# Loading and transposing q and k of the first two head sets in two parts, values sharing a PSUM bank, scrap products ahead, and new instruction orders in a fused attention and MLP kernel

## The chip, the cores and the metric

The kernel runs on one core of a Trainium2 chip. The metric is device time in microseconds (us) of one execution; lower is better. The kernel before has a median of 329.98 us over three runs.

## The reference

```python
def _attn_ref(q, k, v, beacon_k, beacon_v):          # B, H, S, D = 8, 8, 576, 64; 16 beacons
    k_all = np.concatenate([beacon_k, k], axis=2)
    v_all = np.concatenate([beacon_v, v], axis=2)
    scores = 1/sqrt(D) * q @ k_all^T                   # causal over k, beacons always seen
    a = softmax(scores)
    return a @ v_all
def _moe_ref(x, w_in, w_out):                          # 4608 tokens, 512 -> 2048 -> 512
    h = x @ w_in
    g = h * (1.0 / (1.0 + np.exp(-1.702 * h)))
    return g @ w_out
```

The attention output of all heads, as 4608 tokens of 512 values, is the input of the two-layer MLP.

## The kernel before

**Sets and chunks.** A set is four heads of one batch: two sets to a batch, 16 in all. Within a set the four heads run side by side in four strips of TensorE's rows or columns. The scores of a set (keys on partitions, queries along the row; only blocks that the causal mask leaves) have 1664 columns per head. They are made in chunks (`CHUNKS`): `e_qk` writes one chunk to the single PSUM tile `s`, `e_exp` (ScalarE) turns it into weights `E` in SBUF, and the next chunk may overwrite `s` only after that. The blocks on the diagonal are masked by VectorE for the first two sets (`e_mask`, tiles `keep` and `keepb`) and by GpSimd for the later ones.

**Values.** `e_av` multiplies `E` by a tile of ones (`x == 2`, the sums) and by the even and odd value columns (`x` 0 and 1), into one of four PSUM banks `u0` to `u3`, the ring. VectorE transposes the sums (`zt`), takes reciprocals (`rc`), spreads them (`rz`) and scales the values into `xT`, the transposed input of the MLP (`e_norm`). Sets below `EARLY` (the first four) are split into two halves of queries at `HF`; there each of the two value products has a bank of its own in both halves. Later sets share a bank for the two products in their first half.

**MLP.** `e_m1` makes 512 columns of the hidden layer in a ring bank; groups 0 and 1 (256 tokens each) take tanh on ScalarE and a product on VectorE (`e_tanh`, `e_gate`), later groups (512 tokens) take a table function (`e_gelu`). The second layer is `e_m2` for groups 0 and 1 and for the rest seven products in place of eight (`e_prod`), joined by VectorE. ScalarE changes its function table between exponentials and `e_gelu`.

**Loads.** q and k of a set lie in DRAM as four heads of 576 rows. `e_load_qk` brings them in float16 to `qn` or `kn`, 18 rows to a partition, and `e_turn` transposes them to `qT`, `kT` in one VectorE instruction. The loads of q, k, v and both weights are all issued by GpSimd (`pool_load`, with at most 8 in flight: a load waits until the one eight places ahead has landed). The beacons of k (`bkf`) come through SyncE's and ScalarE's queues, are cast to `bkn` and transposed into the first columns of `kT`.

**Order.** Instructions are first recorded as operations, and `ORDER` holds, written out for every engine, the numbers of the operations in the sequence in which they are issued. `Plan.run` only merges these five lists and assigns the ring's banks, for which it uses estimated durations. Each engine works through its list in order and waits on semaphores. The first entries are: loads of k, q of set 0, then k, q of set 1; then the mask tiles on GpSimd; then v and the weights. Chunk 0 is set 0's first half, chunk 1 set 1's first half, chunks 2 to 4 the rest of set 0, 5 to 7 the rest of set 1.

The lines that hold the loads and the transposes:

```python
HF = S // 2                                   # 288
def rows_of(t, s):
    return t[b, Q * hs : Q * hs + Q].rearrange("h (r t) d -> (h r) (t d)", t=TR)   # TR = 18
load_bk(0, 1, (), ("SP", "ACT"))
load_bk(1, HS)
load_qk(0, 1); load_qk(0, 0); load_qk(1, 1); load_qk(1, 0)
```

Of the kernel before, what the change touches and what calls it, by code (L numbers as in the profile page):

```python
# [17 lines left out]
        76, 100, 106, 138, 115, 141, 118, 143, 120, 108, 111, 155, 152, 129, 161, 158, 122, 131, 164, 167, 134, 127,  # L18
        170, 173, 176, 145, 125, 148, 150, 177, 182, 188, 191, 227, 194, 197, 232, 183, 203, 234, 200, 178, 237,
        179, 206, 258, 241, 209, 184, 263, 185, 212, 265, 213, 248, 246, 268, 214, 215, 401, 251, 253, 272, 218,  # L20
        404, 275, 244, 279, 219, 220, 407, 282, 284, 277, 221, 414, 320, 296, 304, 290, 302, 292, 300, 298, 312,
        308, 294, 318, 314, 310, 306, 316, 426, 435, 423, 343, 338, 339, 340, 433, 431, 438, 344, 345, 359, 349,
        341, 464, 346, 350, 351, 352, 354, 574, 355, 429, 360, 361, 577, 356, 362, 357, 372, 365, 583, 474, 477,
        373, 366, 374, 367, 605, 480, 484, 375, 482, 607, 368, 506, 502, 488, 492, 610, 490, 486, 498, 504, 500,
        508, 514, 510, 516, 494, 496, 512, 534, 593, 596, 535, 536, 539, 540, 550, 541, 542, 537, 742, 545, 546,
        547, 548, 603, 745, 551, 552, 553, 599, 601, 619, 622, 748, 555, 556, 557, 558, 561, 755, 625, 627, 629,
        562, 563, 776, 568, 564, 569, 570, 571, 779, 764, 767, 659, 637, 641, 657, 649, 651, 647, 661, 635, 631,
        653, 805, 772, 770, 774, 643, 655, 633, 639, 645, 679, 680, 815, 818, 700, 681, 682, 684, 701, 915, 690,
        685, 686, 691, 692, 702, 918, 687, 693, 695, 703, 696, 924, 821, 823, 697, 698, 706, 946, 825, 707, 713,
        708, 709, 948, 934, 937, 714, 715, 716, 827, 951, 944, 940, 942, 853, 831, 833, 855, 857, 851, 843, 835,  # L30
        837, 847, 839, 845, 829, 849, 841, 1083, 960, 963, 875, 876, 880, 877, 878, 881, 882, 1086, 968, 966, 970,
        883, 1089, 902, 909, 903, 886, 891, 1096, 887, 888, 889, 892, 893, 1117, 904, 894, 905, 896, 897, 1120, 898,
        899, 910, 911, 1105, 1108, 1146, 912, 976, 994, 996, 972, 978, 1000, 992, 982, 974, 998, 990, 984, 988, 980,
        1002, 986, 1256, 1156, 1113, 1111, 1115, 1159, 1025, 1020, 1026, 1021, 1259, 1022, 1027, 1031, 1023, 1028,
        1265, 1164, 1162, 1166, 1041, 1042, 1287, 1036, 1047, 1032, 1048, 1033, 1037, 1038, 1034, 1039, 1289, 1054,
        1055, 1049, 1056, 1043, 1044, 1050, 1292, 1057, 1198, 1172, 1168, 1178, 1184, 1180, 1194, 1170, 1174, 1176,
        1275, 1278, 1182, 1186, 1196, 1188, 1190, 1281, 1301, 1285, 1283, 1304, 1216, 1217, 1221, 1192, 1222, 1227,
        1218, 1223, 1228, 1219, 1224, 1232, 1229, 1233, 1230, 1307, 1311, 1309, 1237, 1327, 1333, 1238, 1243, 1234,
        1244, 1235, 1323, 1239, 1245, 1250, 1251, 1341, 1240, 1246, 1252, 1253, 1337, 1405, 1315, 1331, 1343, 1411,
        1335, 1321, 1403, 1431, 1313, 1325, 1407, 1419, 1317, 1423, 1425, 1319, 1339, 1421, 1409, 1329, 1361, 1413,  # L40
        1366, 1382, 1429, 1362, 1363, 1401, 1367, 1364, 1427, 1368, 1383, 1372, 1369, 1373, 1374, 1375, 1388, 1377,
        1389, 1378, 1390, 1395, 1379, 1384, 1380, 1385, 1391, 1396, 1415, 1397, 1398, 1470, 1454, 1417, 1455, 1449,
        1471, 1450, 1451, 1476, 1452, 1456, 1477, 1457, 1478, 1460, 1461, 1462, 1463, 1465, 1466, 1467, 1468, 1472,
        1479, 1473, 1483, 1484, 1485, 1486,
    ],
    "ACT": [
        1, 3, 77, 79, 103, 101, 107, 109, 112, 153, 156, 130, 159, 162, 132, 165, 168, 135, 171, 174, 189, 192, 228,
        195, 198, 233, 235, 201, 204, 238, 180, 207, 259, 210, 264, 186, 266, 269, 216, 402, 405, 408, 222, 417,
        415, 297, 291, 303, 305, 301, 299, 293, 309, 321, 295, 319, 313, 315, 311, 307, 317, 436, 439, 342, 465,
        468, 575, 578, 584, 587, 606, 608, 503, 507, 489, 491, 493, 487, 499, 505, 509, 515, 517, 495, 501, 511,  # L50
        497, 513, 611, 538, 743, 746, 749, 756, 758, 777, 780, 660, 642, 638, 652, 658, 648, 650, 636, 632, 662,
# [48 lines left out]
        1140, 1142, 1130, 1128,  # L100
    ],
    "SP": [
        0, 2, 4, 5, 6, 7, 83, 84, 85, 86, 88, 89, 90, 91, 181, 93, 94, 95, 96, 187, 217, 223, 348, 364, 371, 377,
        544, 560, 567, 573, 689, 705, 712, 718, 885, 901, 908, 914, 1030, 1046, 1053, 1059, 1226, 1242, 1249, 1255,
        1371, 1387, 1394, 1400, 1459, 1475, 1482, 1488,
    ],
# [89 lines left out]
def kernel(  # L196
# [66 lines left out]
    for t in kT:  # L263
        nc.vector.memset(t[:, NK:, :], 0.0)
# [855 lines left out]
```

The softmax here doesn't subtract the row's maximum and nothing guards it: scores larger than these inputs give would overflow.

## Time and profile before

| what | value |
|---|---|
| three runs | 329.98, 332.08, 329.78 us (median 329.98) |
| the profiled execution, first to last instruction | 328.1 us, granted TensorE clock 1.000 |
| TensorE (PE) busy | 309.3 us, 94% |
| VectorE (DVE) busy | 235.9 us, 72% |
| ScalarE (ACT) busy | 202.0 us, 62% |
| GpSimd (POOL) busy | 114.0 us, 35% |
| written by DMA over the span | mean 88 GB/s, 126 to 209 in the first seven of 40 slices |

The profile gives the span of its execution and no other time for it; the median of the runs is 1.88 us above that span, which is what lies around the first and the last instruction. PE is matrix multiplication, PEld the load of its weights. "L434 PE s" is the product of line 434 that writes tile `s`. Idle time of an engine that is not on the path that sets the end costs nothing.

### The profile page before, as it was taken

What the parts mean: (1) busy time and instruction counts of PE and PEld (TensorE: products, weight loads), DVE (VectorE), ACT (ScalarE), POOL (GpSimd) and SP (SyncE); (2) the same over time, 40 slices, a digit from 0 to 9 for tenths busy, and PEclk for the clock granted to TensorE, in tenths of its full rate; (3) what the DMA queues carried; (4) which work ended last, traced back from release to release, by engine and by line L of the source; (5) the groups of instructions that cost most, each with busy time, mean ns of one, the idle gap of its engine ahead of it and who ended that gap; (6) DMA issues with size and microseconds to landing.
All of it is one profiled execution on the core that took longest, in us unless ns stands there. A gap on an engine that the chain in (4) does not pass through costs nothing.

```text
span 328.1 us, 9811 instructions
## 1 busy us (share of the span) xinstructions
PE 309.3 (94%) x4288; PEld 210.0 (64%) x4288; DVE 235.9 (72%) x478; ACT 202.0 (62%) x236; POOL 114.0 (35%) x178
## 2 busy tenths in 40 slices
PE   0489999999999999999999999999999999999995
PEld 0367665544775467745878878547764776447884
DVE  3657788777987989977998798958557843006674
ACT  1567597687767686679767686868477212674010
POOL 8765487190319312951078019400042000000000
PEclk9999999999999999999999999999999999999999
DMA  7999999194424921693029809600120012000122
GB/s 126 161 202 209 203 187 181 34 99 103 113 67 72 186 50 34 70 191 57 2 45 177 133 2 122 157 0 2 37 96 2 2 34 78 18 0 2 65 98 97
DMA packets 58219, 28.81 MB, mean 88 GB/s; under 512 B 41280, under 2 KB 53568, under 8 KB 58176
## 3 DMA queue, kind: packets, MB, share of 16 engines
q0 software_dynamic: 47552, 18.49, 47.8%
q1 hardware_dynamic: 10560, 9.69, 9.1%
q8 instruction: 33, 0.54, 0.7%
q14 instruction: 10, 0.08, 0.1%
q10 hardware_dynamic: 64, 0.01, 0.0%
HBM read 37.22 MB, written 9.44 MB: 142 GB/s over the span
## 4 chain that ended last, share of the span: by engine, by line
PE 89%; ACT 4%; DVE 3%; DMA 2%; issue 1%; POOL 0%; DVEq 0%; ACTq 0%; POOLq 0%
PE u L580 36%; PE u L694 30%; PE s L434 9%; PE u L521 9%; PE u L625 4%; ACT E L445 3%; DMA qn<-in_q_dram 2%; DVE qT L405 1%; DVE sA L645 1%; DVE xT L556 1%; DVE rz L544 0%; DVE zt L533 0%; ACT L601 0%; DVE osb L710 0%; DVE rc L540 0%
## 5 line engine op out<-in xcount | busy, mean ns | idle before, releaser
L580 PE MATMUL u<-xT,w 128*128 128x512 f16 (+1 forms) x704 | 130.4, 340 | 0.5 <-ACT g L601 0.5
L445 ACT ACTIVATE E<-s 128x2048 f16<-128x2048 f32 (+5 forms) x66 | 98.9, 1515 | 46.0 <-PE s L434 45.6
L601 ACT ACTIVATE g<-u 128x512 f16<-128x512 f32 x128 | 70.5, 598 | 53.8 <-PE u L580 53.4
L580 PEld LDWEIGHTS <-w 128*128 128x128 f16 x704 | 67.8, 98 | 53.9 <-issue 1.5
L466 POOL TENSOR_SCALAR_AFFINE_SELECT E<-E 128x512 f16<-128x512 f16 (+3 forms) x78 | 49.3, 663 | 113.4 <-ACT E L445 81.6
L710 DVE SCALAR_TENSOR_TENSOR osb<-u,osb 128x512 f32<-128x512 f32 x56 | 37.2, 682 | 24.7 <-PE u L694 22.4
L694 PEld LDWEIGHTS <-g 128*128 128x128 f16 x512 | 48.4, 98 | 9.3 <-issue 0.2
L694 PE MATMUL u<-w,g 128*128 128x256 f16 x384 | 50.6, 273 | 0.0
L434 PE MATMUL s<-qT,kT 32*128 32x32 f16 (+20 forms) x1376 | 35.4, 232 | 14.4 <-DVE qT L405 8.4
L434 PEld LDWEIGHTS <-kT 32*128 32x128 f16 x1376 | 25.8, 94 | 30.6 <-issue 15.0
L694 PEld LDWEIGHTS <-sA 128*128 128x128 f16 x384 | 36.3, 98 | 5.3 <-issue 0.3
L694 PE MATMUL u<-tB,sA 128*128 128x256 f16 x256 | 35.0, 273 | 0.1
L645 DVE TENSOR_TENSOR sA<-g 128x512 f16<-128x512 f16 x32 | 12.9, 415 | 26.2 <-ACT g L601 26.2
L556 DVE TENSOR_TENSOR xT<-u,rz 128x352 f16<-128x352 f32 (+2 forms) x52 | 25.6, 517 | 6.9 <-PE u L521 6.7
L365 POOL DMA_DIRECT2D vb<-in_v_dram x32 | 27.4, 874 | 2.3 <-DMA kn<-in_k_dram 1.5
L521 PE MATMUL u<-E,vb 128*32 128x352 f16 (+8 forms) x928 | 28.0, 267 | 0.0
L484 DVE TENSOR_TENSOR zs<-zs,E 128x1344 f16<-128x1344 f16 (+2 forms) x36 | 22.7, 633 | 5.3 <-POOL E L466 4.4
L521 PEld LDWEIGHTS <-vb 128*32 128x32 f16 (+1 forms) x928 | 20.2, 99 | 5.9 <-issue 1.7
L405 DVE STREAM_TRANSPOSE kT<-kn 128x576 f32<-128x576 f32 x16 | 20.1, 1258 | 2.4 <-DMA kn<-in_k_dram 1.6
L405 DVE STREAM_TRANSPOSE qT<-qn 128x576 f32<-128x576 f32 x16 | 19.8, 1239 | 0.1
L533 DVE STREAM_TRANSPOSE zt<-u 128x224 f32<-128x224 f32 (+2 forms) x32 | 14.9, 471 | 6.6 <-PE u L521 6.5
L484 DVE TENSOR_TENSOR zs<-E 128x1856 f16<-128x1856 f16 x12 | 15.8, 1319 | 3.3 <-POOL E L466 3.3
(44 smaller groups left out, 237.7 us busy)
## 6 DMA issues: line engine op xcount, KB each, us to landing
out_dram<-osb SPq DMA_DIRECT2D x36, 256.0 KB, 2.5
kn<-in_k_dram POOLq DMA_DIRECT2D x16, 288.0 KB, 6.7
qn<-in_q_dram POOLq DMA_DIRECT2D x16, 288.0 KB, 6.6
vb<-in_v_dram POOLq DMA_DIRECT2D x24, 128.0 KB, 6.6
w<-in_moe_w_in_dram POOLq DMA_DIRECT2D x8, 256.0 KB, 9.9
w<-in_moe_w_out_dram POOLq DMA_DIRECT2D x4, 512.0 KB, 14.2
vb<-in_v_dram POOLq DMA_DIRECT2D x8, 112.0 KB, 5.0
vb<-in_v_dram POOLq DMA_DIRECT2D x8, 80.0 KB, 7.9
```

What stands on the lines that cost most here:

```text
L365: nc.gpsimd.dma_start(out=t[0 : hi - lo, j, h0:h1, :], in_=v[b, h0:h1, lo:hi, :].rearrange("h n d -> n h d"),)
L405: nc.vector.transpose(out=f32(dst.rearrange("p n e -> p (n e)")).rearrange("p (r t) -> p t r", t=TR), in_=f32(src[:, :]).rearrange("p (t c ...
L434: nc.tensor.matmul(sc[:, h, o : o + w], kT[s % NB2][r : r + 32, j * P : (j + 1) * P, d], qT[s % NB2][r : r + 32, a : a + w, d], start=(d = ...
L445: nc.scalar.activation(out=Es[s][:, :, c0:c1], in_=ss[i][:, :, o : o + c1 - c0], func=AFT.Exp, scale=0.125,)
L466: nc.gpsimd.affine_select(out=blk, in_=blk, compare_op=ALU.is_ge, fill=0.0, base=off + (Nb if j == 0 else 0), pattern=[[0, Q], [1, w]], ch ...
L484: nc.vector.tensor_tensor(out=t, in0=E[:, :, Z0:S] if i == 1 else t, in1=E[:, :, wcol[i] : wcol[i] + S - a], op=ALU.add,)
L521: nc.tensor.matmul(u[32 * h : 32 * h + 32, a:e], lhs, src[0:kw, h, col : col + e - a], start=first, stop=last,)
L556: nc.vector.tensor_tensor(out=xT[:, 2 * hs + x : 2 * hs + x + n, t0 : t0 + w], in0=rings[("av", s, x, half)][:, 0 : n * w].rearrange("p (n ...
L580: nc.tensor.matmul(u[:, o + a - t0 : o + e - t0], w1t[:, kp, nt * P : (nt + 1) * P], xT[:, kp, a % XR : (e - 1) % XR + 1], start=(kp == 0) ...
L601: nc.scalar.activation(out=gts[g][:, n0:n1, 0:w], in_=rings[("m1", g, n0)][:, 0 : n * w].rearrange("p (n w) -> p n w", n=n), func=AFT.Gelu ...
L694: nc.tensor.matmul(u[:, HM * mt : HM * (mt + 1)], lhs[:, n, mt * P : (mt + 1) * P], rhs[:, n, :], start=(n == 0 and mt == 0), stop=(n == H ...
L710: nc.vector.scalar_tensor_tensor(out=osbs[(g, dst)][:, :], in0=rings[("p", g, p)][:, :], scalar=scale_of(g), in1=osbs[(g, src)][:, :], op0 ...
```

## The change

1. `HF` becomes 256. The first half of an early set is queries 0 to 255; for batch 0 these are exactly the tokens of MLP group 0. The four chunks of an early set have 416 columns each (before: 512, 384, 384, 384); the first is taken by two exponentials of 256 and 160 columns. The sum of columns stays 1664.
2. q and k of sets 0 and 1 are loaded and transposed in two parts, rows 0 to 255 and 256 to 575 (`ENDS`). All later sets still come whole.
3. In early sets the two value products of the first half share one ring bank and one `e_norm`, as later sets already did.
4. The beacons of sets 0 and 1 come in one load per head (two on SyncE, two on ScalarE), in place of two.
5. Three float32 products of 512, 384 and 256 columns on made-up numbers in `sA[0]` (filled by two VectorE memsets) go to bank `u3`, which nothing reads before it is written again: two ahead of chunk 0, one between chunk 0 and chunk 1.
6. All lists in `ORDER` are replaced, and the planner's estimates are changed (a flat cost for a change of TensorE's mode, 2200 ns for a store before its buffer is taken again).

```diff
-    HF = S // 2
+    HF = 256
...
-    nc.vector.memset(bkf[:, 0:1, :], 0.0)
-    nc.vector.memset(bkf[:, 1:HS, :], 0.0)
+    nc.vector.memset(bkf[:, 0:HS, :], 0.0)
+    scrap = sA[0][:, 0:4, :].rearrange("p a n -> p (a n)").bitcast(F32)
+    for i, x in enumerate((1.7, -0.6)):
+        nc.vector.memset(scrap[:, i::2], x)
+    nc.vector.memset(ones, 1.0)
     for t in kT:
-        nc.vector.memset(t[:, NK:, :], 0.0)
-    nc.vector.memset(ones, 1.0)
+        nc.vector.memset(t[:, Nb + HF :, :], 0.0)
+    FILL = {"qk0": (512, 384), "qk1": (256,)}
...
+    ENDS = ((0, S), (0, HF), (HF, S))
+
+    def e_load_qk(s, which, part):
         b, hs = divmod(s, HS)
+        a, e = ENDS[part]
         dst = (qn, kn)[which][s % NB3]
-        nc.gpsimd.dma_start(out=dst[:, :], in_=rows_of((q, k)[which], s))
+        nc.gpsimd.dma_start(
+            out=dst[:, a // 32 * D : e // 32 * D],
+            in_=(q, k)[which][b, Q * hs : Q * hs + Q, a:e].rearrange("h (r t) d -> h r (t d)", r=32),
+        )
...
-        if s >= EARLY and half == 0:
+        if x < 2 and half == 0:
...
-        n = 2 if s >= EARLY and half == 0 else 1
+        n = 2 if half == 0 else 1
...
+        if CHUNKS[i][0][0] < HS and CHUNKS[i][0][1] == 0:
+            turned(CHUNKS[i][0][0], 2, [qks[i]])
...
-    load_bk(0, 1, (), ("SP", "ACT"))
-    load_bk(1, HS)
-    load_qk(0, 1)
-    load_qk(0, 0)
-    load_qk(1, 1)
-    load_qk(1, 0)
+    load_bk(0, HS, (), ("SP", "ACT"))
+    for s in range(HS):
+        load_qk(s, 1, part=1)
+        load_qk(s, 0, part=1)
     keeps = op("POOL", 1100, [], e_keep, pr=0, name="keep")
     for j in range(-1, 3):
         load_v(0, j)
     w1_cols(0, 512)
+    for s in range(HS):
+        load_qk(s, 1, part=2)
+        load_qk(s, 0, part=2)
...
+    idle = psu.tile([P, 512], F32, tag="u3", name="u3")
     for o in order:
+        for w in FILL.get(o.name, ()):
+            nc.tensor.matmul(idle[:, 0:w], scrap[:, 0:P], scrap[:, 0:w], start=True, stop=True)
         o.emit()
```

`ORDER` decides where these stand. As the built programs show it, the first instructions of the changed kernel are: on GpSimd q part 1 of set 1, k and q part 1 of set 0, k part 1 of set 1, v block 0, its beacons, q part 2 of set 0, two loads of w1, k part 2 of set 0, v blocks 1 and 2, then the mask tiles, two more loads of w1, and q and k part 2 of set 1. On VectorE, after the memsets: casts of both beacon sets, transposes of q of set 1, k and q of set 0, k of set 1 (parts 1), q part 2 of set 0, two memsets, k part 2 of set 0, and only then the six masks of the first halves, two `zt`, and `rc`, `rz`, `xT` for each set. On TensorE: scrap, chunk 0, scrap, chunk 1, chunk 2, the sums and values of set 0's and set 1's first halves, chunks 3 and 4, then the MLP's first products.

## The prediction

> **What bounds the kernel now.** I read the waits of TensorE first, then the busy time in four stretches, cut at the first score product (8.38), the first MLP product (20.49) and the first MLP product of group 2 (66.26).
>
> ```profile
> PE s L434 <- DVE qT L405: 8.4, 1, 8.4
> PE s L434 <- ACT E L445: 5.7, 3, 2.0
> PE u L580 <- ACT g L601: 0.5, 1, 0.5
> ...
> 0.00:8.38 8.38, 0.00 (x0) 0.10 (x1) 3.38 (x9) 1.28 (x1) 7.15 (x17) 1.00 0.76 128
> 8.38:20.49 12.11, 6.45 (x200) 5.24 (x200) 8.77 (x22) 6.78 (x6) 8.51 (x14) 1.00 1.59 173
> 20.49:66.26 45.77, 45.53 (x884) 30.65 (x873) 34.55 (x65) 33.92 (x35) 26.34 (x44) 1.00 1.19 164
> 66.26:324.30 258.04, 257.29 (x3228) 174.05 (x3216) 188.54 (x383) 160.02 (x195) 71.96 (x107) 1.00 0.42 67
> ```
>
> The first number after the stretch is its length, the next PE's busy time. From 20.49 on PE is never idle for more than 0.5 us: nothing can be won there but PE's own work. All the room is ahead of 20.49. The chain of waits in order of time says what fills it:
>
> ```profile
> 1.96 5.09 DMA qn<-in_q_dram
> 7.07 1.27 DVE qT L405
> 8.38 1.07 PE s L434 x20
> 9.48 1.95 ACT E L445 x2
> 11.47 1.07 PE s L434 x20
> 12.55 1.95 ACT E L445 x2
> 14.54 0.83 PE s L434 x15
> 15.38 2.59 PE u L521 x72
> 17.97 0.52 PE s L434 x24
> 18.51 1.46 ACT E L445
> 20.01 0.55 PE s L434 x29
> 20.56 1.85 PE u L580 x16
> ```
>
> A load, its transpose, then score chunks that alternate with their exponentials. VectorE runs a second path to the same point: masks, sums and `xT`.
>
> ```profile
> 14.53 0.39 DVE L459 TENSOR_TENSOR E<-E,keepb 128x448 f16<-128x448 f16 x1 [0.21 <-ACT E L445]
> 15.98 0.91 DVE L533 STREAM_TRANSPOSE zt<-u 128x288 f32<-128x288 f32 x2 [1.06 <-PE u L521]
> 16.92 0.22 DVE L540 RECIPROCAL rc<-zt 128x9 f32<-128x9 f32 x1
> 17.17 0.48 DVE L544 STREAM_TRANSPOSE rz<-rc 128x288 f32<-128x288 f32 x1
> 19.52 0.82 DVE L556 TENSOR_TENSOR xT<-u,rz 128x288 f16<-128x288 f32 x2
> ```
>
> **What the Trainium skill says.** "TensorE: Matmul & The Clock Gate", Part 1, says that the array starts at half its clock and goes to full only after a window of about 3.4 us in which it was busy. The trace agrees in effect: chunk products take 1.07 us at 8.38 and 11.47 and 0.52 at 17.97, although the clock column reads 1.00 throughout. The same page, in the part on the array's sub-arrays, calls VectorE's queue strictly first in, first out. "FP8 and Floating Point Precision", TensorE Precision Notes, gives true float32 four passes; no float32 product is in this trace. "DMA: Bandwidth & Descriptors", "Two DMAs through the same engine are not ordered", says that descriptors of one queue start in order. Issue plus time to landing agrees: k, q, k, q of the first two sets land at 5.6, 7.1, 8.5 and 10.0.
>
> **Loads.** Those landings lie 1.45 us apart for 288 KB, so 200 KB/us, and a load of no size would land at 5.6 - 1.45 = 4.15. Parts of 128 KB take 0.64: q of set 1 lands at 4.8, k of set 0 at 5.45, q of set 0 at 6.1, k of set 1 at 6.75. Behind them v block 0 and beacons (128 KB in short rows, at the 161 GB/s of the slice where v was loaded: 0.8) reach 7.55, q part 2 of set 0 (160 KB) 8.35, two w1 of 256 KB 9.65 and 10.95, **k part 2 of set 0: 11.75**. Then v blocks 1, 2 13.4, two w1 16.0, q, k part 2 of set 1 17.6.
>
> **Start.** Before: q lands 7.06, turned 8.3, chunk 0 at 8.38. After: a whole transpose costs 1.26, and 32 columns 0.21, so 1.93 ns a column: 256 columns about 0.6, 320 about 0.72. VectorE: set 1's q 4.8-5.4, beacons 0.2, k of set 0 to 6.2, q to 6.75; chunk 0 at 6.8, **1.6 earlier**. Two beacon casts (0.31 and 0.20) end by 4.1, unseen. The memsets grow: 0.17 for `bkf`, two of 256 float32 (0.27 each, the row of the 128x256 memset), two of 368 (0.4 each); about 1.6 in all, to 2.5, also unseen. If none of that were hidden it would cost 1.
>
> **Scrap.** 896 columns x 4 passes / 1.2 GHz = 3.0 us by the skill's figures (an estimate), 1.7 to 4.7, ahead of chunk 0. Bounds: it costs nothing, or, were it twice as long, it would end at 7.7 and delay chunk 0 by 0.9. I take nothing: masks set the pace anyway (next step). Its use: the chunks at half a microsecond. The third (256 columns) lies in the wait for exponential 0.
>
> **Chunks.** Chunk 0 of 416 columns, warm, 0.5; exponentials 1152+896 columns took 1.95, so 1024+640 take 1.95 - 384 x 0.83 ns = 1.63. Exponential 1 ends near 11.2, chunk 2 can follow at once (its q part is turned by 9.1; it needs no k part 2), at 11.3 against 14.54.
>
> **The new wait.** On VectorE k part 2 of set 0 stands ahead of all six masks. It lands at 11.75, is turned by 12.5, and behind it queue masks of 64, 512, 64, 448, 512, 448 columns (0.2, 0.36, 0.2, 0.36, 0.36, 0.39): sums of set 0 at 13.6, the last mask at 14.4. So the masks end only 0.5 earlier than before (14.92), with exponentials done 3 us earlier. From there: `zt` 0.45, `zt` of set 1 (its sums end about 14.8, plus 0.2 for the semaphore) to 15.4, a memset 0.2, `rc` and `rz` 0.7, `xT` of 2x256 columns 0.65, `rc`, `rz` 0.65, `xT` 0.65: 18.3. **First MLP product 18.35 instead of 20.49, 2.1 less.** The shared bank is worth part of that: two `xT` operations, not four. Chunks 3 and 4 and two exponentials of 416 columns (1.57) fit between 14.9 and 18.3.
>
> **PE's work behind it.** By then PE has done five chunks of 416 columns and 2x3x416 of values, where before it had 2176 columns of chunks and 2x3x512: 0.33 us of products are left over for later (columns / 2.4 GHz). Against this the programs' lists show fewer changes between the three kinds of products (row strips, column strips, whole array): from the first MLP product on 128, not 141; 8 fewer before group 2 and 5 behind. In the trace the start-to-start gap across such a change is 0.097 above the product's own time on average: 0.78 and 0.49 saved.
>
> **New stalls.** Between the first MLP products and the second layer chunks follow each other closely. Where chunk 5 to 6 has one MLP product (0.9) and sums (0.55) between, and 6 to 7 only one MLP product, ScalarE must do an exponential (1.57) and a tanh (0.6): about 0.15 and 0.6 of PE waiting; later two tanh ahead of an exponential 0.2, and a gate behind two transposes 0.25. Sum 1.2, against 0.57 of such stalls before in this stretch (two of 0.3 at 36.9 and 39.5). I take +0.9, to leave room for one I did not see; bounds 0 to +2.5. The weights then: w1 loads end at 19, 21.7, 25 and 27.8 by the same rates, each 0.5 us or more before its product; w2 parts land from 33.7 to 41.5, its first product stands at 37.5.
>
> **Rest.** At 66.26 both kernels stand at the same work. Before, PE waits 0.66 at 69.5 for the change of ScalarE's table; after, the long second-layer product stands ahead and the four banks are free: 0.5 saved. The remaining stages have the same columns and the same 14 table loads, and the last 11.4 us the same products, so the 4.1 us behind the last product stay.
>
> **Sum.** -2.14 + 0.33 - 0.78 + 0.9 - 0.49 - 0.5 = -2.7 against the span of 328.1, so about 325.4; the median of the runs lies 1.88 above the span: **327.3**.
>
> **Rivals.**
> The array stays cold. PE is busy 3.0 us, less than the window, and then rests 2 us; before, full clock came only after 3.1 us of unbroken work (14.54 to 17.7). For it: no float32 product was measured here. Against it: the third product and chunks 0 and 1 give a second try. Price: sums and values cold, +0.4, and up to 3.4 us of MLP products at half speed, +1.7: 329.4. Chance 0.18.
>
> k part 2 lands early, or masks wait less than I think, so that exponential 1 (11.2) sets the pace: masks end at 12.6, the MLP starts at 16.6, 1.7 earlier still: 325.6. For it: landings depend on a rate that I took from slices. Against it: the queue's order is strict. Chance 0.22.
>
> Slower: the loads become the bound. PE arrives 2 us earlier at w1 and w2 while the queue's bytes up to w2's second part are unchanged: some 3.8 MB from 17 to 35.3 at 203. Its margin at 37.5 is 1.2 us. Every microsecond lost there is lost by PE, which has nothing else. At 150 KB/us this part takes 25 us, 6.5 more, 5.3 beyond the margin: 332.6 or more; it decides below 160 KB/us. The 161 of one slice speaks for it, the 202 to 209 of slices 3 to 5 against. Chance 0.06.
>
> The new orders stall no longer and no less than said: forecast, chance 0.54.
>
> **How the numbers follow.** Forecast 327.3, own range 326.0 to 328.8 (stalls 0 to 2.5, start 0.5 either way). With 325.6 and 329.4 the range is 325.2 to 330.2; outside lie the slow rival and little more. About 1% (3.3 us) is what the measurement can tell from no change, so faster is below 326.7: nearly all of the second rival and a fifth of the forecast, 0.32; slower above 333.3: half the last rival and some, 0.05; same 0.63.
>
> **What would show it.** Chunk 0 at 6.8 and taking 0.5; VectorE idle until near 11.8 and then k part 2 and the masks; first MLP product (first `u` from `xT`) at 18.3; PE waiting for ScalarE near 22 to 25; group 2 at about 64.2; no 0.66 us gap behind it. It would be wrong if chunks took 1 us until the MLP, if masks ran ahead of 11.7, or if PE had gaps of over 1 us between 20 and 60.

## The result, and the profile after

The changed kernel takes 341.01 us (median of 6 runs, 340.08 to 342.04), the kernel before 330.5 beside it: ratio 1.0313, 95% interval 1.0285 to 1.0341, so 3% slower. The forecast was 327.3. The profiled execution has a span of 339.2 against 328.1, and everything below is summed against these two.

The busy time in four stretches, cut at the first score product (11.09), the first MLP product (23.70) and the first MLP product of group 2 (74.10), as it was read for the kernel before:

```profile
0.00:11.09 11.09, 3.35 (x4) 1.28 (x5) 3.74 (x13) 1.28 (x1) 7.76 (x15) 0.90 0.72 74
11.09:23.70 12.61, 7.80 (x203) 6.32 (x202) 7.71 (x20) 6.35 (x6) 9.54 (x17) 0.50 1.48 170
23.70:74.10 50.40, 47.07 (x883) 31.97 (x874) 35.56 (x66) 35.12 (x35) 28.71 (x46) 0.98 1.19 163
74.10:333.00 258.90, 257.72 (x3217) 173.91 (x3215) 187.60 (x380) 158.88 (x194) 73.37 (x106) 1.00 0.41 64
```

The first two stretches took 8.38 and 12.11 before. In the third, PE's busy time is 47.07 of 50.40, where it was 45.53 of 45.77: TensorE now waits where it never waited, and the last column but two (the granted clock) says 0.50 for the whole second stretch. With the last product's start (323.96 before, 332.68 after) and the span this gives the account of the loss:

| stage | before | after | difference | forecast |
|---|---|---|---|---|
| to the first MLP product | 20.49 | 23.70 | +3.21 | -2.14 |
| to the first MLP product of group 2 | 45.77 | 50.40 | +4.63 | +0.45 |
| to the last product's start | 257.70 | 258.57 | +0.87 | -0.99 |
| to the end of the span | 4.12 | 6.54 | +2.42 | 0 |
| sum | 328.1 | 339.2 | +11.1 | -2.7 |

(+0.45 is 0.33 of work, less 0.78 for fewer changes of kind, plus 0.9 of stalls; -0.99 the other changes of kind and the table gap.)

The start, from VectorE in order of time (start, duration, what; in brackets its idle time and what ended it):

```profile
6.99 0.64 DVE L414 STREAM_TRANSPOSE qT<-qn 128x256 f32<-128x256 f32 x1 [3.01 <-DMA qn<-in_q_dram]
8.71 0.64 DVE L414 STREAM_TRANSPOSE kT<-kn 128x256 f32<-128x256 f32 x1 [1.06 <-DMA kn<-in_k_dram]
10.40 0.64 DVE L414 STREAM_TRANSPOSE qT<-qn 128x256 f32<-128x256 f32 x1 [1.06 <-DMA qn<-in_q_dram]
...
11.41 0.64 DVE L414 STREAM_TRANSPOSE kT<-kn 128x256 f32<-128x256 f32 x1 [0.35 <-DMA kn<-in_k_dram]
...
16.55 0.75 DVE L414 STREAM_TRANSPOSE kT<-kn 128x320 f32<-128x320 f32 x1 [1.80 <-DMA kn<-in_k_dram]
17.14 0.56 DVE L468 TENSOR_TENSOR E<-E,keep 128x64 f16<-128x64 f16 x3
```

Every transpose waits for its load. The first three loads land 1.7 us apart and the fourth 1.0 behind them, though each has 128 KB; 288 KB took 1.45 before. Masks stand right behind k part 2, at 17.1. On TensorE:

```profile
22.88 0.88 PE L443 MATMUL s<-qT,kT 32*128 32x208 f16 x32 [1.67 <-ACT E L454]
23.70 2.98 PE L590 MATMUL u<-xT,w 128*128 128x256 f16 x16
```

A chunk still takes 0.88 at 22.88, and sixteen MLP products take 2.98 where later blocks of sixteen take 1.92: the array was cold, at half its clock, until 25.90. (The chain of waits, which carried the reading of before, does not help here: its longest pieces all begin behind 175.) What TensorE waited for in the whole span (us in total, times, longest):

```profile
PE s L443 <- DVE kT L407: 6.1, 1, 6.1
PE s L443 <- ACT E L454: 4.7, 4, 1.7
...
PE u L531 <- issue: 1.4, 1, 1.4
PE u L531 <- DVE E L468: 0.8, 1, 0.8
PE u L635 <- DMA w<-in_moe_w_out_dram: 0.8, 2, 0.4
```

The last three are new. The first sums and values wait 0.8 for masks, and second-layer products wait 0.8 for their weights. In the 1.4 us of "issue", from 67.5 on, TensorE stands among the value products of set 3 and waits for nothing that the profile shows (see fill67 and the last section). The packet counts of the two pages, first before, then after:

```profile
DMA packets 58219, 28.81 MB, mean 88 GB/s; under 512 B 41280, under 2 KB 53568, under 8 KB 58176
```

```profile
DMA packets 61803, 28.82 MB, mean 85 GB/s; under 512 B 44352, under 2 KB 57664, under 8 KB 61760
```

Of the 3584 new packets 512 are the rows of four more loads. 3072 are under 512 B: 384 packets of 4 bytes for each of the eight part loads, beside the 16 that every load has.

At the end, the joins and stores of the last outputs:

```profile
330.37 3.33 DVE L720 SCALAR_TENSOR_TENSOR osb<-u,osb 128x512 f32<-128x512 f32 x5 [0.18 <-PE u L704]
331.48 1.47 PE L704 MATMUL u<-w,sA 128*128 128x256 f16 x12
333.13 2.22 SPq L727 DMA_DIRECT2D out_dram<-osb  x4
```

Five joins run without a pause and four stores are issued from 333.13 to 334.91. The last join ends 1.0 behind the last product's start, as before; its store is issued 1.2 later (before: 0.03), and the span ends 4.3 after that (before: 3.1).

### The profile page after: what moved, and what is told of

The parts are those of the page before. It is cut to its first block, busy times and chain, and to the rows that moved or that the text cites. A ratio compares the mean times of both kernels' runs of the same rounds, so it can differ in the third digit from the quotient of the medians.

```text
span 339.2 us, 9800 instructions
## 1 busy us (share of the span) xinstructions
PE 315.9 (93%) x4294; PEld 213.5 (63%) x4294; DVE 235.3 (69%) x479; ACT 201.6 (59%) x236; POOL 119.4 (35%) x182
## 5 line engine op out<-in xcount | busy, mean ns | idle before, releaser
L475 POOL TENSOR_SCALAR_AFFINE_SELECT E<-E 128x512 f16<-128x512 f16 (+2 forms) x78 | 51.4, 679 | 75.7 <-ACT E L454 75.6
L443 PE MATMUL s<-qT,kT 32*128 32x32 f16 (+17 forms) x1376 | 36.0, 235 | 11.1 <-DVE kT L407 6.1
L531 PE MATMUL u<-E,vb 128*32 128x352 f16 (+9 forms) x928 | 28.5, 267 | 1.7 <-issue 1.4
L566 DVE TENSOR_TENSOR xT<-u,rz 128x352 f16<-128x352 f32 (+3 forms) x48 | 25.2, 545 | 2.3 <-PE u L531 1.9
L531 PEld LDWEIGHTS <-vb 128*32 128x32 f16 (+1 forms) x928 | 21.1, 98 | 7.5 <-issue 3.2
L414 DVE STREAM_TRANSPOSE kT<-kn 128x576 f32<-128x576 f32 (+2 forms) x18 | 20.4, 1133 | 7.0 <-DMA kn<-in_k_dram 6.4
L493 DVE TENSOR_TENSOR zs<-zs,E 128x1344 f16<-128x1344 f16 (+2 forms) x36 | 23.7, 668 | 2.0 <-POOL E L475 1.4
L414 DVE STREAM_TRANSPOSE qT<-qn 128x576 f32<-128x576 f32 (+2 forms) x18 | 20.2, 1124 | 6.2 <-DMA qn<-in_q_dram 5.7
L543 DVE STREAM_TRANSPOSE zt<-u 128x352 f32<-128x352 f32 (+3 forms) x32 | 14.7, 467 | 6.4 <-PE u L531 6.4
L704 PE MATMUL u<-tB,g 128*128 128x256 f16 x128 | 18.6, 273 | 0.0
```

The lines of the kernel that those rows point to most:

```text
L414: nc.vector.transpose(out=f32(dst.rearrange("p n e -> p (n e)")).rearrange("p (r t) -> p t r", t=n), in_=f32(src[:, a // 32 * D : e // 32 ...
L443: nc.tensor.matmul(sc[:, h, o : o + w], kT[s % NB2][r : r + 32, j * P : (j + 1) * P, d], qT[s % NB2][r : r + 32, a : a + w, d], start=(d = ...
L475: nc.gpsimd.affine_select(out=blk, in_=blk, compare_op=ALU.is_ge, fill=0.0, base=off + (Nb if j == 0 else 0), pattern=[[0, Q], [1, w]], ch ...
L493: nc.vector.tensor_tensor(out=t, in0=E[:, :, Z0:S] if i == 1 else t, in1=E[:, :, wcol[i] : wcol[i] + S - a], op=ALU.add,)
L531: nc.tensor.matmul(u[32 * h : 32 * h + 32, a:e], lhs, src[0:kw, h, col : col + e - a], start=first, stop=last,)
L566: nc.vector.tensor_tensor(out=xT[:, 2 * hs + x : 2 * hs + x + n, t0 : t0 + w], in0=rings[("av", s, x, half)][:, 0 : n * w].rearrange("p (n ...
```

## The experiments

Each edit is against the changed kernel unless it says otherwise. Ratios are to the kernel before, run on the same chip; spans are of one profiled execution. The six executions of the changed kernel have spans of 338.4 to 340.3, and the intervals of flat, whole, noscrap, fill67, tail281 and start_all overlap with that of the changed kernel (1.0285 to 1.0341). Where such a run differs by one or two us, it is the place in the trace that tells, not the total. In a list of operation numbers square brackets hold what was put in, round ones what was taken from there.

### The loads

**flat.** The source of the part loads makes one evenly strided dimension.

```
-  in_=(q, k)[which][b, Q * hs : Q * hs + Q, a:e].rearrange("h (r t) d -> h r (t d)", r=32),
+  in_=(q, k)[which][b, Q * hs : Q * hs + Q].rearrange("h (r t) d -> (h r) (t d)", t=TR)[:, a // 32 * D : e // 32 * D],
```

> The changed kernel, with the parts of the first two sets' q and k read from another place: the same 128 and 160 KB, the same rows of 1024 and 1280 bytes to the same partitions, but a source in which head and row make one evenly strided dimension (part 1 is the first 8 rows of every 18, as the whole load of before reads them). q and k rows of these two sets are thereby permuted; nothing else differs. Theory P (the part loads are slow because of their source, whose two outer dimensions do not merge: each of them carries 384 packets of 4 bytes more than a whole load): those packets go, landings come 0.64 to 0.9 apart from near 5, chunk 0 stands at 6.8 to 7.8 and, 2 to 3 us behind the scrap products, still has the full clock (0.5 us), the first MLP product comes at 18.3 to 19.5, and the span falls by 5 to 9, to 330 to 334. Theory S (parts of this size simply take 1.5 us each, since a row of 1024 bytes costs an engine nearly what one of 2304 does): landings within 0.5 of those of the changed kernel, chunk 0 at 10.6 to 11.1 and cold, span 338 to 340.

Ratio 1.0256 (1.0205 to 1.0308), span 337.6. VectorE:

```profile
4.63 0.64 DVE L414 STREAM_TRANSPOSE qT<-qn 128x256 f32<-128x256 f32 x1
5.33 0.64 DVE L414 STREAM_TRANSPOSE kT<-kn 128x256 f32<-128x256 f32 x1
6.82 0.64 DVE L414 STREAM_TRANSPOSE qT<-qn 128x256 f32<-128x256 f32 x1 [0.85 <-DMA qn<-in_q_dram]
```

The small packets are gone (58731 in all, 3072 fewer), the first loads land near 4.6, 5.2, 6.8 and 7.4, and chunk 0 stands at 7.50, 3.6 earlier. So theory P holds for the landings. It fails for the rest: the chunks still take 0.90 (the scrap did not warm the array here), k part 2 is turned at 14.37, the first MLP product comes at 21.52, and only 1.6 us of span are won.

**b_pat.** The kernel before, with the same form of source at the whole size.

```
-  return t[b, Q * hs : Q * hs + Q].rearrange("h (r t) d -> (h r) (t d)", t=TR)
+  h = t[b, Q * hs : Q * hs + Q] if s >= HS else t[b, hs::2]
+  return h.rearrange("h (r t) d -> h r (t d)", t=TR)
```

> The kernel before, with q and k of the first two sets read from every second head (heads 0, 2, 4, 6 for set 0, 1, 3, 5, 7 for set 1, so other heads than the reference's; times alone count): whole loads of 288 KB and 2304 bytes a row as before, but head and row no longer merge into one dimension of the source. Theory P (such a source costs by itself, at any size: 384 packets of 4 bytes more per load, and a late start of its data): 1536 packets more, landings at 6.5 to 7.5 and then 2 or more apart where before has 5.6 and 1.45; chunk 0 at 10 to 12 for 8.4; first MLP product 1.5 to 3 later; span 329.5 to 331.5. Theory S (it hurts parts alone, whose rows are short): landings within 0.3 of before, span within 0.5 of 328.1.

Ratio 1.0193 (1.0150 to 1.0236), span 336.7. Exactly 1536 packets more (59755), four times 384. VectorE's first two transposes:

```profile
11.70 1.25 DVE L406 STREAM_TRANSPOSE kT<-kn 128x576 f32<-128x576 f32 x1 [7.75 <-DMA kn<-in_k_dram]
13.82 1.26 DVE L406 STREAM_TRANSPOSE qT<-qn 128x576 f32<-128x576 f32 x1 [0.86 <-DMA qn<-in_q_dram]
```

Before they stood at 5.70 and 7.07. Theory P, and more than it priced: such a source delays the first landing by 6 us, at rows of 2304 bytes as well. From 2.5 to 6.0 the DMA moved 42 GB/s, where the kernel before moved 165. The first MLP product is 7.4 late (27.88), one cold block of products adds 1.2, and these 8.6 reach the end of the span whole, since the rest of the kernel is unchanged. This execution is the slowest of its four; the median of the runs is 6.5 above that of the kernel before.

**whole.** The parts undone.

```
-    ENDS = ((0, S), (0, HF), (HF, S))
+    ENDS = ((0, S), (0, S), (HF, S))
+        if part > 1:     # ahead of the load and of the transpose
+            return
```

> The changed kernel with the parts undone, all else as it is: the first load of each of the four q and k fetches all 576 rows with the source of before, its transpose turns all of them, and the second loads and transposes are left out. Order of landings as before: 5.6, 7.1, 8.5, 10.0, for q of set 1, k of set 0, q of set 0, k of set 1. Theory L (late loads are behind the start and the stalls up to the first layer of group 2): chunk 0 at 9.9 to 10.5, cold; masks right behind the exponentials, first MLP product at 20.5 to 21.5, group 2 at 68 to 70 (before 66.3, after 74.1), span 332 to 335. Theory O (the new orders stall by themselves between the first MLP product and group 2, 4.6 us more than before): first MLP product as said, but group 2 at 72 to 74 and span 336 to 338. In both the tail stays 2.4 longer than before.

Ratio 1.0258 (1.0211 to 1.0304), span 339.1, that of the slowest of four executions (340.79 us, median 339.3): the runs put it beside flat. The first MLP product comes at 22.02, 1.7 earlier, but group 2 at 73.49, after 51.5 us (50.4 in the changed kernel). Theory O is right that the new orders stall without late parts; its own span was 1 to 3 too low. The longest wait in that stretch grew to 2.3, and behind it the array was back at half clock from 67.59 to 71.00, which with TensorE busy throughout costs some 1.7 of the 51.5 (an estimate, half of these 3.41 us):

```profile
PE s L447 <- ACT E L458: 2.4, 2, 1.7
PE u L535 <- issue: 2.3, 1, 2.3
PE u L639 <- DMA w<-in_moe_w_out_dram: 1.1, 1, 1.1
```

### The array's clock

**noscrap.** `FILL = {}`: no scrap products.

> The changed kernel without the five scrap products and nothing else. Theory N (the scrap warmed the array at 5.4, but the first chunk came at 11.1, after it had gone cold at 8.8, so it is worth nothing): same time within 0.5, chunk 0 still 0.9, full clock from near 25.9 in both. Theory H (the products themselves do harm, by standing ahead of chunks 0 and 1 or by shifting the window in which the clock is decided): 0.6 to 1.5 us faster, with the clock full earlier. Theory W (the third product helps): slower by 0.5 to 1.

(It says five products; `FILL` lists three, which are six records in the profile.)

Ratio 1.0322 (1.0270 to 1.0375), 341.4 us: theory N, no difference from the change. In the clock record of the changed kernel the array is full from 5.42 to 8.84 and then half until 25.90; chunk 0 came at 11.09.

**b_scrap.** The kernel before with longer scrap.

```
+    scrap = sA[0][:, 0:4, :].rearrange("p a n -> p (a n)").bitcast(F32)
+    for i, x in enumerate((1.7, -0.6)):
+        nc.vector.memset(scrap[:, i::2], x)
+    FILL = {"qk0": (512, 384, 512, 512, 512, 256), "qk1": (512,), "qk2": (256,)}
     nc.vector.memset(bkf[:, 0:1, :], 0.0)
```

> The kernel before with scrap products alone added, long enough to last to its first chunk: 2688 columns of float32 ahead of chunk 0 (1.7 to 8.1 by 3.35 us for 896 columns cold and half of that per column once warm), 512 ahead of chunk 1 and 256 ahead of chunk 2. Theory W (a warm array is worth what the cold chunks cost): chunks 0, 1 and 2 take 0.5, 0.5 and 0.4 where they took 1.07, 1.07 and 0.83, values and sums 1.7 for 2.6; the chain alternates chunks and exponentials, so the first MLP product comes 1.5 to 2 us earlier, at 18.5 to 19, and the span falls by 1.3 to 2, to 326 to 326.8. Theory D (VectorE's path to the first MLP product binds, masks, zt and xT, and these do not depend on the array): first MLP product at 19.8 to 20.4 and span within 0.7 of before.

Ratio 1.0015 (0.9990 to 1.0041), a miss of my own making. The two scrap memsets stood ahead of the memset that the beacon loads wait for: SyncE issued its first beacon load at 1.57 instead of 1.03, the beacons were in at 5.96 instead of 3.32, k of set 0 was turned at 6.64 instead of 5.70, and the first MLP product came at 22.09.

**warm.** The kernel before with scrap, its operand written last.

```
     nc.vector.memset(ones, 1.0)
+    scrap = ...
+    for i, x in enumerate((1.7, -0.6)):
+        nc.vector.memset(scrap[:, i::2], x)
+    FILL = {"qk0": (512, 384, 512, 256), "qk1": (512, 128), "qk2": (512,), "av1.2.0": (256,)}
```

> The kernel before with scrap products alone added, this time with their operand written after everything that the beacons and transposes wait for: 1664 columns of float32 ahead of chunk 0, 640 ahead of chunk 1, 512 ahead of chunk 2 and 256 ahead of the first sums. Theory W (a warm array is worth its cold chunks): loads and transposes as in before, chunks 0 to 2 at 0.55 to 0.65 us, first MLP product at 18.7 to 19.5, span 326.3 to 327.3, runs 0.3 to 0.5 per cent below before. Theory D (VectorE and ScalarE set the pace up to the first MLP product, and the clock falls back between the chunks): first MLP product at 20 to 20.5, no difference.

Ratio 0.9968 (0.9953 to 0.9984), 329.67 us over 22 runs: faster than the kernel before, by a third of a per cent. Its profiled span, 328.1, does not show it. Full clock from 5.34 to 8.75, half to 12.16, then full to 329.6; chunk 0 took 1.04, chunks 1 and 2 0.65 and 0.54; first MLP product at 20.20. Between the two theories: the runs gain what W said, at the lower end, and the first MLP product stands where D said. In this execution it is 0.29 earlier and group 2 only 0.04: behind the sixth MLP product TensorE stops for 0.22.

**best.** Whole loads, the orders of before (the run oldord_whole below) and the same scrap.

> The run with whole loads and the orders of before (the shared bank is all that was left of the change), and the same scrap products as in the run before this one. If the bank's 0.3 and the warm array add up: first MLP product at 18.3 to 19.2, span 326 to 327, the fastest of all runs here by 1 to 2 us of its profiled span. If the array falls back to half clock between the chunks: 19.6 to 20, span 327.6 to 328.2, and no difference in the runs.

Ratio 0.9982 (0.9962 to 1.0001), span 327.8. Here the array was full from 4.55 on; chunks took 0.57 and the first MLP product came at 18.69, 1.8 before that of the kernel before. Group 2 began at 65.72, 0.5 before. Most of the rest was given back at once:

```profile
18.69 0.83 PE L590 MATMUL u<-xT,w 128*128 128x256 f16 x6
20.37 1.25 PE L590 MATMUL u<-xT,w 128*128 128x256 f16 x10 [0.85 <-issue]
```

From 18.69 to group 2 TensorE waits for no load. Of the 1.3 us given back 1.0 is this stop, between the starts of two products; the other 0.25 oldord_whole gives back too (46.02 for 45.77 in this stretch).

### The orders

**oldord.** The changed kernel's operations in the orders of before: only the lists of operation numbers differ.

> The changed kernel with its parts, its shared bank and its scrap, but with the orders of before on every engine (each operation at the place that it has in the kernel before; the second parts' loads behind the first two weight loads, their transposes behind the six masks of VectorE; the products that the shared bank makes needless are dropped). Theory O (the new orders are behind most of the loss: VectorE's k part 2 ahead of the masks, the stalls between the first MLP product and group 2, the tail): loads stay late (1.7 apart), chunk 0 at 9 to 9.6, first MLP product at 20.5 to 21.5, from there to group 2 45.5 to 46.5 as in before (50.4 in the changed kernel), tail 4.1, span 328 to 331. Theory L (late loads and a cold array are behind it, the orders only show it): first MLP product at 22 to 23.5, group 2 another 49 to 50 later, span 334 to 337.

Ratio 1.0214 (1.0166 to 1.0262), span 336.9. The start was worse than either theory, as I had put the second parts' loads behind the first two weight loads: k part 2 was turned at 19.56 and the first MLP product came at 27.51. Behind it the orders show clean: 47.2 to group 2, of which a cold block is 1.2; from there to the last product 257.71, before 257.70; tail 4.4. Theory O for all that lies behind the first MLP product.

**oldord_whole.** The same with whole loads and no scrap.

> As the run with the orders of before, and besides whole loads and transposes (the second ones left out) and no scrap: what is left of the change is the shared bank of the first values, two operations of VectorE ahead of the first MLP product for four, and the cut of a set's first score part at 256 columns instead of 288. Theory B (the bank is worth its two operations' fixed cost, some 0.2 us each on VectorE's path): first MLP product at 20.0 to 20.4, span 327.2 to 328, runs 0 to 0.9 below before. Theory C (the new cut costs as much: the second score chunks and exponentials become longer): span 328 to 329, no difference.

Ratio 1.0005 (0.9985 to 1.0025), span 328.0. First MLP product at 19.90, 0.6 earlier, group 2 at 65.92, 0.3 earlier. What the bank brings is too little for the runs to tell.

**fill67.** Two pieces of second-layer products ahead of the values of set 3.

```
 PE:  ... 407, 279, 274, [222, 223,] 282, 277, 284, 414, (222, 223,) 224, 225, ...
```

> The changed kernel with two pieces of the second layer of group 1 (eight products of 512 columns, 1.7 us) taken out from behind the next score chunk and put ahead of the values of set 3 on TensorE, so that they lie in its wait for the mask of 68.2 to 68.9; nothing else. Theory O (the 1.7 us there are an order that leaves TensorE nothing to do while ScalarE and GpSimd finish the last chunk's exponential and mask): the wait at 67.2 shrinks from 1.69 to under 0.3, group 2 starts at 72.4 to 72.8 instead of 74.1, and the span falls by 1.2 to 1.7. Theory M (the next score chunk and exponential move back by the 1.8 us of the products put ahead, and TensorE waits for them later): group 2 within 0.5 of 74.1, or the same microseconds lost by 110; span within 0.4.

Ratio 1.0282 (1.0235 to 1.0329), span 337.7. Theory O for the time: the eight products fill the wait,

```profile
65.90 0.90 PE L528 MATMUL u<-E,ones 128*32 128x320 f16 x32
66.74 1.90 PE L632 MATMUL u<-w,g 128*128 128x512 f16 x8
68.57 1.81 PE L528 MATMUL u<-E,vb 128*32 128x320 f16 x64
```

group 2 starts at 72.62, 1.5 earlier, and the span keeps all of it. The new order had all values of sets 2 and 3 stand in one row behind their score chunks; that of before has second-layer products between them.

But the wait was not for the mask that the expectation names. First the changed kernel, then noscrap:

```profile
66.81 0.66 PE L531 MATMUL u<-E,vb 128*32 128x320 f16 x15
68.91 1.22 PE L531 MATMUL u<-E,vb 128*32 128x208 f16 x49 [1.43 <-issue]
```

```profile
66.95 0.81 PE L531 MATMUL u<-E,vb 128*32 128x320 f16 x21
68.75 1.11 PE L531 MATMUL u<-E,vb 128*32 128x256 f16 x43 [0.99 <-issue]
68.37 0.63 POOL L475 TENSOR_SCALAR_AFFINE_SELECT E<-E 128x512 f16<-128x512 f16 x1 [4.69 <-ACT E L454]
```

In noscrap the wait ends 0.25 before the mask does, and with six product records fewer ahead of it, it stands six products further on (21 for 15). With six more (start_all) it stands behind 9. It belongs to a place in TensorE's program, not to an operand.

**tail281.** The orders of before for the last operations.

> The changed kernel with the orders of before for its last operations alone (all that before begins in its last 40 us, group 8's first layer and what follows), the rest as it is. Theory T (the longer end is the new order of the last products, which makes four outputs ready within 1.9 us, so that their joins queue on VectorE and their stores on SyncE): from the last product's start to the end of the span 4.0 to 4.4 instead of 6.5, stores issued 0.7 to 0.9 apart, span 336.5 to 337.5. Theory D (stores land later for another reason, 2.7 after their issue instead of 1.8): 5 to 6.5 as now, span 338 to 339.5.

Ratio 1.0246 (1.0194 to 1.0298), span 337.0. Theory T: 4.4 behind the last product's start, last stores issued at 332.02, 332.75 and 333.61.

**w2early.** The four loads of the second weights ahead of three masks (139, 142, 143) on GpSimd, and so of a load of v and one of q (69, 59).

```
 POOL:  ... 57, 47, [51, 49, 63, 61,] 139, 69, 59, 142, 143, (51, 49, 63, 61,) 71, ...
```

> The changed kernel with the four loads of the second weight matrix moved on GpSimd from behind three masks to ahead of them, so that they are issued from 28.4 on and not from 34.6; nothing else. Theory Q (in the new order they queue on GpSimd behind masks that wait for exponentials, and land only when TensorE needs them): the waits at 44.2 (0.71) and 49.5 (0.53) shrink to those of a change of kind, 0.1 to 0.2, group 2 starts 0.7 to 1.0 earlier, at 73.1 to 73.4, span 338.2 to 338.5. Theory R (all loads of this stretch share one rate, and what is moved forward pushes the others back): the waits move to the score chunks of sets 2 and 3, whose q and k come later, group 2 within 0.4 of 74.1 or later.

Ratio 1.0578 (1.0542 to 1.0614), span 348.3. Theory R, and far dearer than I had thought: 9.1 us of span. The waits between 36 and 60:

```profile
DVE qT L411 <- DMA qn<-in_q_dram: 8.7, 1, 8.7
PE u L587 <- DVE g L620: 7.8, 1, 7.8
...
ACT sig L601 <- DVE g L620: 6.0, 1, 6.0
```

A load of q, now behind 2 MB of weights, kept VectorE waiting 8.7 us in front of its transpose; the gates behind it could not run, and the tanh and TensorE waited for the gates. After TensorE's wait the array was at half clock from 47.53 to 54.36, which costs some 1.7 of the 9.1 (half of the 3.40 us in which TensorE was busy there).

### The start as predicted

**flat_masks.** flat, and the transpose of k part 2 (81) behind the six masks on VectorE.

```
 DVE:  ... 88, 98, (81,) 113, 86, 87, 84, 112, 110, [81,] 124, ...
```

> The changed kernel with the evenly strided source of the part loads (the run above; q and k rows of the first two sets permuted) and one more edit: on VectorE the transpose of k part 2 of set 0 stands behind the six masks, not ahead of them. Theory W (the masks wait for that load, and the first MLP product waits for the masks): in the run above k part 2 is turned at 14.4 to 15.1 and the exponentials of the first two sets were done at 12.7; the masks move to 12.8 to 14.2, the values and the third score chunk some 2 us forward, the first MLP product from 21.5 to 19.5 to 20.3, and the span falls by 1.2 to 2. Theory P (the chain of chunks and exponentials sets the pace: chunk 3 needs k part 2 and comes behind it anyway): first MLP product at 21 to 21.6, span within 0.5.

Ratio 1.0244 (1.0208 to 1.0281), span 336.3. The masks did move to 12.1 to 13.7, but the first MLP product stayed at 21.66, for TensorE's wait for masks (2.2 in flat) turned into a wait for v:

```profile
PE u L528 <- DMA vb<-in_v_dram: 1.9, 2, 1.1
```

Theory P's number, not its reason. Of the 1.3 us of span won nothing is at the first MLP product, and the ratios do not tell this run from flat.

**start_all.** flat_masks, with v ahead of k part 2 and of the weights, and scrap up to chunk 0.

```
-POOL:  10, 4, 6, 8, 15, 13, 27, 21, 23, 25, 17, 19, 12, ...
+POOL:  10, 4, 6, 8, 15, 13, 27, 17, 19, 12, 25, 21, 23, ...
-    FILL = {"qk0": (512, 384), "qk1": (256,)}
+    FILL = {"qk0": (512, 384, 512), "qk1": (512,), "qk2": (512,), "av0.2.0": (256,)}
```

> The changed kernel with the start as the prediction assumed it: evenly strided source of the part loads (rows of q and k of the first two sets permuted), VectorE's six masks ahead of k part 2, blocks 1 and 2 of v and the mask tiles ahead of k part 2 and of the first weights on GpSimd's queue, and scrap products long enough to last to the first chunk (1408 columns, then 512, 512 and 256). Theory I (the idea holds once its costs are right): chunks of 0.56, masks done by 13.2, v landed by 12, first MLP product at 17.5 to 18.7, 3 below the run with the source alone, span 333 to 334.5. Theory N (the next thing is late at once: weights, which now land at 13.5 to 15, the chain of exponentials, or VectorE's path): first MLP product at 19.5 to 21.5, span 335 to 337.5.

Ratio 1.0301 (1.0245 to 1.0358), span 338.9. The array is warm up to there (full from 6.97 to 20.62), chunks take 0.57, and the first MLP product stands at **17.40**, better than the 18.35 predicted. Theory I at that point, and theory N for the kernel: group 2 starts at 74.07, where it started in the changed kernel (74.10). All 6.3 us are gone. TensorE between 17 and 45, those lines that had a wait:

```profile
20.70 1.46 PE L587 MATMUL u<-xT,w 128*128 128x256 f16 x6 [1.84 <-issue]
23.45 0.88 PE L440 MATMUL s<-qT,kT 32*128 32x320 f16 x24 [1.28 <-DVE qT L411]
25.20 1.46 PE L587 MATMUL u<-xT,w 128*128 128x256 f16 x6 [0.33 <-DMA w<-in_moe_w_in_dram]
29.89 0.57 PE L440 MATMUL s<-qT,kT 32*128 32x208 f16 x32 [0.71 <-ACT E L451]
44.64 0.61 PE L632 MATMUL u<-w,g 128*128 128x512 f16 x2 [1.89 <-DMA w<-in_moe_w_out_dram]
```

Half of the 6.3 is loads: a part of set 1's q and k that came late (k is turned at 22.08 after 4.3 us of waiting for its load), first weights, second weights. TensorE's waits for these three are 4.1 us in this stretch, 1.0 in the changed kernel. The stop of 1.84 is no wait for data that the profile shows. And the array fell back to half clock:

```profile
20.62:27.45 6.83, 5.13 (x54) 2.68 (x58) 1.92 (x4) 2.64 (x3) 3.52 (x6) 0.50 1.39 197
```

Its 5.13 us of work there, for 2.20 at half clock in the changed kernel (23.70 to 25.90), cost some 1.5 (half the difference).

**sum3.** flat, fill67 and tail281 together.

> The changed kernel with three of the edits above at once: the evenly strided source of the part loads (q and k rows of the first two sets permuted), the two pieces of second-layer products in the wait for the mask, and the orders of before for the last operations. If the three are separate losses they add up: 339.2 - 1.6 - 1.5 - 2.2 = 333.9, first MLP product at 21.5, no wait of over 0.3 at the values of set 3, 4.4 behind the last product; span 333.4 to 334.4. If they hide one another (a stall filled in one place comes back in another): 335 to 336.

Ratio 1.0142 (1.0100 to 1.0184), span 332.4, 1.5 below the sum of the three. They don't hide one another; the rest is luck with the array's clock, which no edit touched and which in this execution was full from 19.56 on, so that its first sixteen MLP products, with the score chunk behind them, took 2.35 where they took 3.87 in flat. What is left against before is 1.3 at the first MLP product, 1.9 from there to group 2, 0.9 to the last product and 0.3 in the tail. In the 1.9 TensorE waits 0.7 for an exponential, 0.6 for a late load of q and 0.4 at a stop like that of fill67; it no longer waits for weights.

## Why the prediction was wrong

**Loads: the first step that failed.** It priced a part by its bytes, 0.64 for 128 KB at the rate of whole loads. Measured: 1.7 (once 1.0) with the source that the change uses, and 0.6 to 1.6 with an evenly strided one. The form of the source was not looked at. It alone costs some 2.4 us at the first landing with 128 KB (6.99 for 4.63 in flat) and 6 with 288 KB (b_pat). Even with the good source the queue behind was priced too low: k part 2 of set 0 was turned at 14.4, not landed at 11.75.

**Start and chunks.** Chunk 0 at 6.8: measured 11.09, and 7.50 with the source mended. "Chunk 2 at 11.3": 16.37.

**Scrap.** Its length was right (3.35 for 3.0), and that it costs nothing (noscrap). Its use was not: 3.35 us of work is too short. The Trainium skill, "TensorE: Matmul & The Clock Gate", Part 1, calls the activity window free-running; all lengths in the clock records here, but for the last of each, are multiples of 3.413 us, so work of that length seldom fills a whole window. Nine kernels here have the change's scrap; the changed kernel alone went to full clock by it, and its window ended 2.2 us before chunk 0. The rival "the array stays cold" named this, at 0.18.

**The new wait.** Right in kind: masks right behind k part 2, TensorE's values behind the masks. But it was not the only one. With it gone (flat_masks) v's load set the same time.

**What the first MLP product is worth.** "From 20.49 on PE is never idle [...]: nothing can be won there but PE's own work. All the room is ahead of 20.49." So an earlier start was counted whole. start_all had the start that was forecast, and a better one, and won nothing by group 2: of its 6.3 some 3.1 went to waits for loads, 1.8 to a stop and 1.5 to half clock. In the new order the loads came just in time for a late start, with no time to spare for an early one. The slower rival had this half (loads become the bound), with a margin of 1.2 and a chance of 0.06. In the orders of before the sentence did better: best came to the first MLP product 1.8 earlier and kept 0.5, but 1.0 of the 1.3 lost is the stop, and none of it a load. What the start would be worth there without the stop is not shown.

**New stalls.** Taken as +0.9, bounds 0 to 2.5. The stretch got 4.63 longer. The array was cold for one block of products (+1.06), which the forecast had only as a rival. Five gaps between starts, at 30.1, 33.3, 44.2, 49.5 and 67.2, make 4.4 together, 3.9 without the 0.1 that each would take anyway; before there were 0.6. With 0.33 of work and the 0.78 of fewer changes that is 3.9 of the 4.63; the other 0.7 was not followed further. The exponential and tanh of the forecast are the gap of 0.97 at 30.1. The two gaps at 44 and 49 come from the second weights: the forecast had them land from 33.7 to 41.5, but GpSimd issued all four between 34.6 and 37.6, behind masks that waited for exponentials (before: two of them at 17.1 and 17.8). Of a moved order every queue that it passes counts; I had followed VectorE's and TensorE's and priced GpSimd's by its bytes. That an earlier place would have mended it is not shown: the one tried (w2early) made it worse. In sum3, which issues them from 31.6 on, TensorE does not wait for them. The gap at 67.2, 1.69 of the stretch, was not seen at all; fill67 shows that another order fills it, and what TensorE waits for there is the last section's question.

**Rest and tail.** The 0.66 behind the table change did go, but gaps of 0.49 and 0.62 came at 129 and 133: +0.87 where -0.99 was forecast. The two gaps are not all of that difference, and no run takes the rest apart. "The 4.1 us behind the last product stay": 6.5, from the order of the last joins and stores (tail281), though the products were the same.

So of the 11.1 us, in single executions, the mended source takes 1.6 of span, two orders 1.5 and 2.2, and a warm block, by luck, some 1.5. What stays in sum3, 4.3, is 1.3 at the start, 1.9 in the stretch behind it and 1.2 after group 2's start; no run parts it further.

## What to carry to other kernels

Before pricing a smaller load, look at whether the dimensions of its source still merge into as few as before; bytes alone do not tell. A stretch in which the bottleneck engine never waits is not proof of slack in its supplies (start_all): before counting on an earlier start, list for each load in that stretch when it lands and when it is used, and look for long rows of short products, in front of which TensorE may stop (fill67). And when all orders change, read each queue's new list to the end, the stores' and the loads' too.

## What the hardware showed that was not expected

A load of 128 rows from a source with two outer dimensions that do not merge carries 400 packets of 4 bytes where others carry 16, and the first such load landed 6 us late (b_pat). What these packets do is not shown here; in flat, without them, the DMA moved 130 GB/s from 2.5 to 6.0, in the changed kernel 47.

Scrap before the kernel before's own first chunk is worth 0.3% once it lasts 4.8 us (warm); on the profiled execution nothing of it is seen at group 2, where the stop that ended at 21.27 had taken most of it.

In warm, best and start_all TensorE stopped for 0.22, 0.85 and 1.84 us at the same place of its program, behind its 222nd product, in the middle of products that waited on no semaphore there. In all three a fetch of 16 KB of instructions had begun 2.2 to 2.4 us before the stop ended (19.04 and 21.27; 17.96 and 20.37; 18.41 and 20.70). The wait at 67.2 is of the same kind: it stands some 768 products and six fetches further on, in eight kernels with the new order, and ends 2.2 to 2.5 us after a fetch began (66.50 and 68.91 in the changed kernel). The two places are 128 products to a fetch apart. Counted in steps of 128 from the 222nd, one step to each fetch, in none of the 17 kernels does the product behind a step start less than 2.2 us after its fetch began; fill67, which does not stop at the second place, passes it 2.20 behind. So it is the place in the program that stops TensorE, and a row of short products reaches it early. That TensorE waits for the fetch itself fits every run, but no run alters a fetch alone: it is argued, not shown.
